# Attention and token-mixing kernel: order of the first q products, of one block's row scaling and of the hand-over to the MLP

## The chip, the cores and the metric

The kernel runs on one core of a Trainium2 chip. The metric is the device time of one execution in microseconds (us), as the median of several runs. Five engines with queues of their own take part: TensorE (PE, with its weight loads PEld), VectorE (DVE), ScalarE (ACT), GpSimd (POOL) and SyncE (SP), which here issues all transfers.

## The reference

For x of 2048 tokens by 640 channels, the output is a gated mix of an attention with 32 heads of width 20 that share one k and one v, and a token-mixing MLP.

```python
S, D, H, Dh, F = 2048, 640, 32, 20, 1728
g = sigmoid((x * gate_w).sum(-1, keepdims=True))
q = (x @ wq) split into 32 heads;  k = x @ wk;  v = x @ wv
a = softmax(q @ k.T * Dh**-0.5) @ v, heads joined, @ wo
h = layernorm(x)                         # over the channels
u = gelu(h.T @ w1 + b1)                  # (D, F): along the tokens
b = (u @ w2 + b2).T
out = g * a + (1 - g) * b
```

## The kernel before, in words

Every float32 operand of a product is split into a high part, which is rounded, and a low part, the rest; a product is then three matmuls (high by high, high by low, low by high). Engines run their instructions in exactly the order in which the source issues them (`manual_schedule`), so each line's place in the Python is its place in the queue. Waits between engines come from the tiles: a reader waits for the writer, and a new user of a buffer waits for the last reader of the old one, transfers included.

**Projection stage (to about 101 us).** Four blocks `sb` of 512 tokens. `load_x` fills `xin[sb % 2]` (tiles `xa`, `xb`). `transpose_x` (L269) turns each of the five column blocks `c` of x on TensorE; `split_x` (L264) makes its high part on ACT and its low part on VectorE. `project` (L276) forms k, v and the gate's sum in one group (`wkv_s`, ten matmuls) and then five q tiles `m` of 128 columns, 15 matmuls each. `split_q` (L290) splits a finished q tile, ACT first and VectorE behind it, into `qh` and `ql`, buffers of the pool `paw` with two of each, and stores both to `q_scr` in memory. It is called one q tile late (`due`). `layer_norm(sb)` (L220) is a generator that the q loop advances with `next`: statistics on VectorE, the reciprocal root partly on GpSimd, and then for each of four row tiles a scaled `ht` on VectorE (L244, pool `tmp`, two buffers), its high part on ACT (L248) and its low part on GpSimd (L249).

Block 0 has its own start, `first_block` (L344). While x and the weights still arrive column block by column block, `turn(c)` casts the weights on GpSimd, transposes and splits x; `first_q` (L340) adds the high-weight products of column block `c` to the first three q tiles at once (`ahead`), three matmuls with the high part of x (`j = 0`) and three with the low part (`j = 1`). `turn(c + 1)` stands in front of `first_q(c, ...)`. Six matmuls on a constant, at L182, come first of all. `gates()` (L328) turns the gate's sums of all four blocks into the columns that the output stage uses: one exponential on ACT and five small VectorE operations.

**First MLP stage (about 101 to 175 us).** The pool `psb` is opened, and ten of the 28 tiles of the first MLP product run (`pu`, L557), in 160 chunk steps of six matmuls. Between them `lead()` issues pairs of products `ms` (L447) whose row maxima VectorE takes (`mp`, L450); softmax needs them. There are 48 leads, spread evenly from step `skip` on:

```python
at, skip, last = 0, 5, NS * PRO - 6
done = [max(0, min(x, last) - skip) * LEAD // (last - skip) for x in (at, at + 1)]
```

A finished tile goes through `gelu` (L483), whose steps are handed out one per chunk step by `pop_chain`. The products `ms` use PSUM banks that the projection stage's `pp` tiles had, and the tile `yo` of `gelu` lies where pool `pa`, with `xin`, had been. `w1_upto` (L112) loads the MLP's weights (`wr`) and splits them on ACT (`wh`, L121) and GpSimd (`wl`, L124).

**Long loop (from about 175 us).** Scores, exponentials, the value product, the other 18 tiles of the first MLP product, the whole second one and the output projection are interleaved by hand. The diff doesn't touch it.

Of the kernel before, what the change touches and what calls it, by code (L numbers as in the profile page):

```python
# [10 lines left out]
F32R = mybir.dt.float32r  # L11
# [6 lines left out]
P = 128  # L18
S, D, H, DH, F = 2048, 640, 32, 20, 1728
NS = S // P  # L20
DC = D // P
FC = (F + P - 1) // P
FT = F - (FC - 1) * P
HD2 = D // 2
NB = 512
NQB = S // NB
NQ = H // 4
NU = NQB * NQ
PRO = 10
# [8 lines left out]
def mix_kernel(ctx: ExitStack, tc: tile.TileContext, A_x, A_wq, A_wk, A_wv, A_wo,  # L38
               B_x, B_w1, B_b1, B_w2, B_b2, gate_w, out):
    nc = tc.nc  # L40
# [3 lines left out]
    def f32(ap):  # L44
        return ap.bitcast(F32)
# [11 lines left out]
    kst = const.tile([P, S], F32R, name="kst")  # L57
# [108 lines left out]
    with tc.tile_pool(name="pa", bufs=1) as pa, \  # L166
# [5 lines left out]
        xin = [pa.tile([P, 4, D], F32, name=name) for name in ("xa", "xb")]  # L172
# [7 lines left out]
        warm = psa.tile([P, NB], F32, name="pp")  # L180
# [39 lines left out]
        def layer_norm(sb):  # L220
            blk = [xts[4 * sb + i] for i in range(4)]
            st4 = paw.tile([P, 4, 2, 6], F32, name="st4")
            mv = paw.tile([P, 4, 2], F32, name="mv")
            for i in range(4):
                for j in range(2):
                    nc.vector.bn_stats(st4[:, i, j, :], blk[i][:, j * HD2:(j + 1) * HD2])
                nc.vector.bn_aggr(mv[:, i, :], st4[:, i])
                if i % 2:
                    yield
            ve = paw.tile([P, 4], F32, name="ve")  # L230
            r0 = paw.tile([P, 4], F32, name="r0")
            r1 = paw.tile([P, 4], F32, name="r1")
            rstd = paw.tile([P, 4], F32, name="rstd")
            nc.vector.tensor_scalar_add(ve, mv[:, :, 1], EPS)
            nc.gpsimd.tensor_tensor(r0, ve, mhalf, op=ALU.pow)
            yield
            nc.vector.tensor_mul(r1, r0, r0)
            nc.vector.tensor_mul(r1, r1, ve)
            nc.vector.tensor_scalar(r1, r1, -0.5, 1.5, op0=ALU.mult, op1=ALU.add)
            nc.vector.tensor_mul(rstd, r0, r1)  # L240
            for i in range(4):
                st = 4 * sb + i
                ht = tmp.tile([P, D], F32, name="ht")
                nc.vector.tensor_scalar(ht, blk[i], mv[:, i, 0:1], rstd[:, i:i + 1],  # L244
                                        op0=ALU.subtract, op1=ALU.mult)
                for d in range(2):
                    hd = ht[:, d * HD2:(d + 1) * HD2]
                    nc.scalar.activation(h_hi[d][:, st, :], hd, AF.Copy)  # L248
                    nc.gpsimd.tensor_sub(h_lo[d][:, st, :], hd, f32(h_hi[d][:, st, :]))  # L249
                yield  # L250

        xT = {}
# [35 lines left out]
                    [(wq_lo[:, c, cols], ts[c][0]) for c in (0, 3, 1, 4, 2)]]  # L288

        def split_q(sb, m, pp):  # L290
            qh = paw.tile([P, NB], F32R, name="qh")
            ql = paw.tile([P, NB], F32R, name="ql")
            nc.scalar.activation(qh, pp, AF.Copy)
            nc.vector.tensor_sub(ql, pp, f32(qh))
            for j, t in enumerate((qh, ql)):
                nc.sync.dma_start(out=q_scr[j, m * P:(m + 1) * P, sb * NB:(sb + 1) * NB], in_=f32(t))
# [43 lines left out]
        def first_q(c, j, ahead):  # L340
            for m, pp in enumerate(ahead):
                nc.tensor.matmul(pp, wq_hi[:, c, m * P:(m + 1) * P], xT[0, c][j], start=c == 0 and j == 0, stop=False)  # L342

        def first_block():  # L344
            ahead = [psa.tile([P, NB], F32, name="pp") for _ in range(QW // P)]

            def turn(c):
                nc.gpsimd.tensor_copy(wq_hi[:, c, :QW], wqs[c])
                split_x(*transpose_x(0, (c,))[0])

            turn(0)
            for c in range(DC):
                if c + 1 < DC:
                    turn(c + 1)
                for j in range(2):
                    first_q(c, j, ahead)
                wq_low(c, slice(0, QW), wqs[c])
            load_x(1)
            split_wkv()
            for c in range(DC):  # L360
                nc.scalar.activation(wq_hi[:, c, QW:], wqs2[c], AF.Copy)
            for c in (0, 3, 1, 4, 2):
                wq_low(c, slice(QW, D), wqs2[c])
            norm = layer_norm(0)
            for _ in range(3):
                next(norm)
            return ahead, norm

        due = None
        for sb in range(NQB):  # L370
            ahead, norm = first_block() if sb == 0 else ([], layer_norm(sb))
            ts = [xT[sb, c] for c in range(DC)]
            pk = project([(wkv_s[:, c, :], t) for c in range(DC) for t in ts[c]])
            if due:
                split_q(*due)
            kv, k_hi, k_lo = split_kv(pk)
            if 0 < sb < NQB - 1:
                load_x(sb + 1)
            store_k(sb, k_hi, k_lo)
            if sb:  # L380
                next(norm)
            for m in range(DC):
                turned = []
                if sb + 1 < NQB and m > 1 and (sb, m) != (2, DC - 1):
                    turned = transpose_x(sb + 1, ((0, 1), (2, 3), (4,))[m - 2])
                p = q_parts(m, ts)
                if m < len(ahead):
                    pp = project(p[2], ahead[m])
                elif m < DC - 1:
                    pp = project(p[0] + p[1] + p[2])  # L390
                else:
                    pp = project([p[r][c] for c in range(DC) for r in range(3)])
                if m:
                    split_q(*due)
                due = sb, m, pp
                if m == 0:
                    turn_v(sb, kv)
                for t in turned:
                    split_x(*t)
                if sb == 1 and m == 1:  # L400
                    turn_bias()
                if sb == 1 and m == 0:
                    w1_load(3)
                if sb == 2 and 0 < m < 4:
                    w1_upto(m)
                if sb == 3 and m == 1:
                    w1_upto(4)
                    new_qmax(0)
                if sb == 3 and m == 2:
                    gates()  # L410
                for _ in range(1 + (sb and m > 1 or sb == 3)):
                    next(norm, None)
            if sb == 2:
                for t in transpose_x(3, (4,)):
                    split_x(*t)
# [118 lines left out]
            f()  # L534

    with tc.tile_pool(name="psb", bufs=2, space=PSUM, side="right") as psb:
        at, skip, last = 0, 5, NS * PRO - 6
        one_by_one[0] = True

        def lead():  # L540
            for b in range(2):
                ms_next(b)()
            ms_done()

        for fc in range(PRO):
            pu = [psb.tile([P, NB], F32, name=f"pu{r}") for r in range(2)]
            for hf in range(4):
                w1_upto(4 * fc + hf + 4)
                if fc and q_parts_due:
                    q_parts_due.pop(0)()  # L550
                wh, wl = w1t.pop(4 * fc + hf)
                for c in range(HS):
                    st = hf * HS + c
                    for k, (w, h) in enumerate(((wh, h_hi[0]), (wh, h_lo[0]), (wl, h_hi[0]))):
                        for r in range(2):
                            rows = slice(64 * r, 64 * r + 64)
                            nc.tensor.matmul(pu[r][:, :HD2], w[rows, c, :], h[rows, st, :],  # L557
                                             start=(st == 0 and k == 0), stop=(st == NS - 1 and k == 2))
                    done = [max(0, min(x, last) - skip) * LEAD // (last - skip) for x in (at, at + 1)]
                    if done[1] > done[0]:  # L560
                        lead()
                    at += 1
                    pop_chain()
                if fc == 1 and hf == 0:
                    new_q(0)
                if fc == PRO - 2 and hf == 2:
                    assert not q_parts_due
                    one_by_one[0] = False
                    fetch_max(0)
            gelu(0, fc, pu)  # L570
            if fc == PRO - 3:
                store_max(0)
# [28 lines left out]
    last = {"half": None, "ins": None, "sig": None}  # L601
# [272 lines left out]
    for i, (steps, rest, done) in enumerate(seq):  # L874
        item, j = divmod(i + 1, 5)
        rest.insert(0, lambda c=4 * (PRO + item) + (48 * j // 5) // 12: w1_upto(c + 4))
    b2 = [b2_jobs(st) for st in range(NS)]
    m = len(seq)
# [105 lines left out]
    for c in range(CUT // P, DC):  # L984
        r = min(P, HEAD - c * P)
        for st in held:
            oT, _ = room(8 + st - (NS - 4))
            for d in range(2):
# [3 lines left out]
                for k, (j, w) in enumerate(((0, wo_hi), (1, wo_hi), (0, wo_lo))):  # L992
                    nc.tensor.matmul(accs[st, d][:, :HD2], oT[:r, j, c, :], w[:r, c, d * HD2:(d + 1) * HD2],
                                     start=(k == 0 and c == CUT // P), stop=False)
# [4 lines left out]
    for i in range(4):  # L999
        st = NS - 4 + i  # L1000
        for d in range(2):
            at = pp_pool.tile([P, NB], F32, name="p")
# [34 lines left out]
```

## Time and profile before

| | before |
|---|---|
| runs | 1703.98, 1704.21, 1705.4 us |
| median | 1704.21 us |
| profiled execution | 1706.32 us |
| its span, first to last instruction | 1704.5 us |
| mean granted TensorE clock | 0.998 |
| instructions | 39051 |

The span is the profiled execution's time without what lies in front of the first and behind the last instruction, 1.8 us. In the profile `L244` is a line of the kernel's source; a row of the timeline gives the start in us, the duration in us, the engine, the line, the operation, `out<-in` with shapes, the count, and in brackets the idle time of the engine before it with what ended it.

### The profile page before, as it was taken

How to read it: one execution, taken by the hardware profiler on the slowest of the kernel's cores; microseconds unless marked ns; L12 is line 12 of the kernel's file. 1: busy time of each engine (PE TensorE's matmuls, PEld its weight loads, DVE VectorE, ACT ScalarE, POOL GpSimd, SP SyncE). 2: the span in 40 equal slices, each digit the busy share in tenths (PEclk: the TensorE clock that was granted, in tenths of full speed). 3: DMA queues.
4: the chain of work that ended last, by engine and by line, in shares of the span. 5: the costliest groups of instructions: out<-in, count | busy, mean ns of one | idle time of the engine just before them, and what ended most of it. 6: DMA issues, size and time to landing. Idle time of an engine off the chain costs nothing.

```text
span 1704.5 us, 39051 instructions
## 1 busy us (share of the span) xinstructions
PE 1693.6 (99%) x14863; PEld 1105.1 (65%) x14863; DVE 1433.5 (84%) x2915; ACT 1189.2 (70%) x2322; POOL 571.0 (34%) x723
## 2 busy tenths in 40 slices
PE   8999999999999999999999999999999999999998
PEld 6889766666666666666666666666666666555666
DVE  5679888888888988888888888888888888888734
ACT  4445577777777777777777777777777777777775
POOL 5467645444444444322222212222221111111200
PEclk9999999999999999999999999999999999999999
DMA  6655322222222222121122222221111222345411
GB/s 187 207 166 144 107 59 69 60 72 70 58 70 64 74 61 75 51 57 53 46 68 70 67 62 62 62 56 54 55 47 41 62 62 64 88 116 145 131 56 57
DMA packets 173377, 135.45 MB, mean 79 GB/s; under 512 B 32729, under 2 KB 139382, under 8 KB 173190
## 3 DMA queue, kind: packets, MB, share of 16 engines
q1 hardware_dynamic: 173190, 132.96, 27.8%
q8 instruction: 117, 1.92, 0.5%
q14 instruction: 70, 0.57, 0.1%
HBM read 100.27 MB, written 31.65 MB: 77 GB/s over the span
## 4 chain that ended last, share of the span: by engine, by line
PE 94%; issue 2%; DVE 2%; DMA 1%; ACT 1%; POOL 0%; SPq 0%; POOLq 0%; DVEq 0%; ACTq 0%
PE o L640 30%; PE s L613 18%; PE ms L447 17%; PE g L685 12%; PE g L848 8%; PE pu L557 3%; PE pp L281 3%; PE g L797 2%; PE ms L754 1%; PE pp L342 0%; DVE mp L450 0%; PE pt L273 0%; ACT slot L248 0%; DMA xa<-in_A_x_dram 0%; PE g L754 0%
## 5 line engine op out<-in xcount | busy, mean ns | idle before, releaser
L450 DVE TENSOR_REDUCE mp<-ms 128x1 f32<-128x512 f32 x2048 | 1278.4, 684 | 170.2 <-PE ms L447 167.7
L616 ACT ACTIVATE p<-s 128x512 f32<-128x512 f32 x2048 | 1069.1, 604 | 397.4 <-PE s L613 393.8
L447 PE MATMUL ms<-kst,qmx 60*128 60x512 f32 x2048 | 848.5, 421 | 1.7 <-DVE mp L450 0.9
L613 PE MATMUL s<-qst,kst 62*128 62x512 f32 x2048 | 745.3, 404 | 0.0
L640 PE MATMUL o<-p,v_sb 128*32 128x512 f32 x4096 | 554.9, 604 | 0.0
L447 PEld LDWEIGHTS ms<-kst,qmx 60*128 60x128 f32 x2048 | 379.4, 185 | 214.7 <-DVE flag L626 182.8
L613 PEld LDWEIGHTS s<-qst,kst 62*128 62x128 f32 x2048 | 378.0, 186 | 11.5 <-issue 10.9
L848 PE MATMUL g<-slot,wh 64*128 64x320 f32 x1152 | 281.3, 318 | 0.0
L124 POOL TENSOR_TENSOR wl<-wr,wh 128x512 fp32r<-128x512 f32 (+1 forms) x176 | 221.3, 1260 | 34.4 <-ACT wh L121 17.9
L123 POOL CAST wh<-wr 128x512 fp32r<-128x512 f32 (+1 forms) x136 | 79.9, 588 | 445.9 <-PE g L685 282.5
L848 PEld LDWEIGHTS g<-slot,wh 64*128 64x128 f32 x1152 | 190.5, 184 | 59.9 <-DVE flag L626 59.9
L685 PE MATMUL g<-slot,wh 64*128 64x320 f32 x864 | 209.0, 317 | 0.0
L685 PE MATMUL g<-u,wh 64*128 64x320 f32 x864 | 208.9, 317 | 0.0
L640 PEld LDWEIGHTS o<-p,v_sb 128*32 128x32 f32 x4096 | 93.7, 108 | 137.6 <-issue 130.3
L848 PE MATMUL g<-slot,wl 64*128 64x320 f32 x576 | 179.3, 311 | 0.0
L685 PEld LDWEIGHTS g<-slot,wh 64*128 64x128 f32 x864 | 142.3, 184 | 40.2 <-DVE flag L626 40.2
L685 PEld LDWEIGHTS g<-u,wh 64*128 64x128 f32 x864 | 142.2, 184 | 40.3 <-DVE flag L626 40.3
L685 PE MATMUL g<-slot,wl 64*128 64x320 f32 x432 | 134.9, 313 | 0.0
L685 PE MATMUL g<-u,wl 64*128 64x320 f32 x432 | 134.8, 312 | 0.0
L848 PEld LDWEIGHTS g<-slot,wl 64*128 64x128 f32 x576 | 106.0, 184 | 15.1 <-DVE flag L626 15.1
L685 PEld LDWEIGHTS g<-slot,wl 64*128 64x128 f32 x432 | 79.5, 184 | 13.4 <-DVE flag L626 13.4
L685 PEld LDWEIGHTS g<-u,wl 64*128 64x128 f32 x432 | 79.5, 184 | 13.4 <-DVE flag L626 13.4
(191 smaller groups left out, 1416.8 us busy)
## 6 DMA issues: line engine op xcount, KB each, us to landing
wr<-in_B_w_dram SPq DMA_DIRECT2D x152, 256.0 KB
qmx<-q_scr SPq DMA_DIRECT2D x192, 80.0 KB
qst<-q_scr SPq DMA_DIRECT2D x192, 80.0 KB
q_scr<-qh SPq DMA_DIRECT2D x20, 256.0 KB
q_scr<-ql SPq DMA_DIRECT2D x20, 256.0 KB
y_scr<-yo SPq DMA_DIRECT2D x16, 320.0 KB
slot<-o_scr SPq DMA_DIRECT2D x16, 320.0 KB
o_scr<-oh SPq DMA_DIRECT2D x124, 40.0 KB
```

The costliest lines, as they stand in the source:

```text
L123: nc.gpsimd.tensor_copy(wh, wr)
L124: nc.gpsimd.tensor_sub(wl, wr, f32(wh))
L281: nc.tensor.matmul(pp, w, t, start=first and n == 0, stop=not more and n == len(steps) - 1)
L447: nc.tensor.matmul(ms, qmax[n][64 * b:64 * b + 60, pr, qt * P:(qt + 1) * P], kst[64 * b:64 * b + 60, kq * NB:(kq + 1) * NB], start=True, s ...
L450: nc.vector.tensor_reduce(mtiles[n][:, c, kq:kq + 1], ms, axis=AX.X, op=ALU.max)
L557: nc.tensor.matmul(pu[r][:, :HD2], w[rows, c, :], h[rows, st, :], start=(st == 0 and k == 0), stop=(st == NS - 1 and k == 2))
L613: nc.tensor.matmul(s, kst[64 * b:64 * b + 62, kb * P:(kb + 1) * P], q[64 * b:64 * b + 62, pr, :], start=True, stop=True)
L616: nc.scalar.activation(p, s, AF.Exp, scale=SCALE)
L640: nc.tensor.matmul(o[32 * hh:32 * hh + 32, :], v_sb[:, kb, :], ptiles.pop((u, hh)), start=(kb == 0), stop=(kb == NS - 1), skip_group_check ...
L685: other_tile(half, nc.tensor.matmul(hold["p"][:, :HD2], w[r, fc % HS, :], u[d][r, fc, :], start=(hold["n"] == 1), stop=(hold["n"] == 6 * F ...
L797: other_tile(half, nc.tensor.matmul(hold["p"][:, :HD2], o[r, c, :], w[r, c, d * HD2:(d + 1) * HD2], start=(hold["n"] == 1), stop=(hold["n" ...
L848: other_tile(half, nc.tensor.matmul(hold["p"][:, :HD2], w[r, st % HS, :], h[d][r, st, :], start=(hold["n"] == 1), stop=(hold["n"] == 6 * NS)))
```

## The change

It has four parts.

1. In `first_block`, for column block 0 only, two more matmuls on the constant and then the three products `first_q(0, 0)` are issued ahead of `turn(1)`; only `first_q(0, 1)` stays behind it.
2. In `layer_norm` of block 0, `ht` of row tile `i + 1` is made at the end of step `i`, behind the ACT and GpSimd instructions of tile `i`. The other blocks keep their order.
3. The last q tile (block 3, `m = 4`) is split into the first two rows of `xin[0]` in place of buffers of `paw`, and `gates()` is called at `m == 3` in place of `m == 2`.
4. `skip` is 3 in place of 5, so the 48 leads spread over 151 steps rather than 149 and begin two steps earlier.

```diff
@@ layer_norm
-            for i in range(4):
-                st = 4 * sb + i
+            hts = []
+
+            def scaled(i):
                 ht = tmp.tile([P, D], F32, name="ht")
                 nc.vector.tensor_scalar(ht, blk[i], mv[:, i, 0:1], rstd[:, i:i + 1],
                                         op0=ALU.subtract, op1=ALU.mult)
+                hts.append(ht)
+
+            ahead = sb == 0
+            if ahead:
+                scaled(0)
+            for i in range(4):
+                if not ahead:
+                    scaled(i)
                 for d in range(2):
-                    hd = ht[:, d * HD2:(d + 1) * HD2]
+                    hd = hts[i][:, d * HD2:(d + 1) * HD2]
+                    st = 4 * sb + i
                     nc.scalar.activation(h_hi[d][:, st, :], hd, AF.Copy)
                     nc.gpsimd.tensor_sub(h_lo[d][:, st, :], hd, f32(h_hi[d][:, st, :]))
+                if ahead and i < 3:
+                    scaled(i + 1)
                 yield
@@ split_q
-            qh = paw.tile([P, NB], F32R, name="qh")
-            ql = paw.tile([P, NB], F32R, name="ql")
+            if (sb, m) == (NQB - 1, DC - 1):
+                qh, ql = (xin[0][:, i, :NB].bitcast(F32R) for i in range(2))
+            else:
+                qh = paw.tile([P, NB], F32R, name="qh")
+                ql = paw.tile([P, NB], F32R, name="ql")
@@ first_block
             for c in range(DC):
+                if c == 0:
+                    for i in range(2):
+                        nc.tensor.matmul(warm, kst[:, :P], kst[:, :NB], start=True, stop=True)
+                    first_q(c, 0, ahead)
                 if c + 1 < DC:
                     turn(c + 1)
-                for j in range(2):
+                for j in range(c == 0, 2):
                     first_q(c, j, ahead)
@@ the q loop
-                if sb == 3 and m == 2:
+                if sb == 3 and m == 3:
                     gates()
@@ the first MLP stage
-        at, skip, last = 0, 5, NS * PRO - 6
+        at, skip, last = 0, 3, NS * PRO - 6
```

## The prediction

> **What bounds the kernel now.** I read the page first: span and busy time by engine.
>
> ```profile
> span 1704.5 us, 39051 instructions
> PE 1693.6 (99%) x14863; PEld 1105.1 (65%) x14863; DVE 1433.5 (84%) x2915; ACT 1189.2 (70%) x2322; POOL 571.0 (34%) x723
> ```
>
> TensorE is busy for 1693.6 of 1704.5 us. So time can be lost or won in only two ways: PE waits, or PE works at a lower clock. Second view: for whom PE waited in the first 200 us, which hold every line the diff touches.
>
> ```profile
> PE pp L281 <- ACT xT_hi L266: 1.4, 1, 1.4
> PE pt L273 <- DMA xa<-in_A_x_dram: 1.0, 1, 1.0
> PE ms L447 <- DVE mp L450: 0.9, 2, 0.6
> PE ms L447 <- DVE ql L294: 0.7, 1, 0.7
> PE pp L281 <- DVE xT_lo L267: 0.3, 1, 0.3
> ```
>
> The columns are total, times, longest. The waits are few and single: one at the start for x (1.0), one for the fifth column of the second x block (1.4 + 0.3), one for the last q tile (0.7), and 0.9 for the running row maxima. The diff has a part for each of the first three. Third view: busy time and granted clock by stretch.
>
> ```profile
> 2.60:6.02 3.42, 2.61 (x9) 1.71 (x7) 0.14 (x1) 0.60 (x1) 1.69 (x5) 1.00 0.84 252
> 6.02:9.43 3.41, 3.24 (x10) 2.76 (x11) 1.25 (x2) 0.60 (x1) 2.41 (x4) 1.00 1.07 323
> 32.25:42.44 10.19, 8.44 (x30) 5.98 (x29) 6.18 (x13) 3.88 (x9) 3.10 (x4) 0.83 0.80 219
> 33.33:36.74 3.41, 1.66 (x7) 0.81 (x6) 2.03 (x5) 2.29 (x5) 1.68 (x2) 1.00 0.32 116
> 36.74:40.15 3.41, 3.41 (x9) 2.64 (x10) 2.49 (x7) 1.22 (x2) 0.62 (x1) 0.50 1.08 235
> 58.98:65.23 6.25, 6.25 (x30) 4.83 (x28) 3.34 (x8) 2.01 (x4) 1.57 (x2) 1.00 0.82 258
> 214.00:1500.00 1286.00, 1286.00 (x11349) 799.72 (x11349) 1140.50 (x2333) 946.09 (x1846) 409.29 (x541) 1.00 0.23 63
> ```
>
> After the stretch's limits and length come busy times of PE, PEld, DVE, ACT and POOL, then the clock. From 214 to 1500 us PE has no idle time and the full clock, so what is gained ahead of 214 us arrives at the end undiminished. And the 1.7 us wait near 35 us costs more than itself: PE is busy for only 1.66 of the 3.41 us up to 36.74, and the next 3.41 us run at clock 0.50, that is, 1.71 us of work is lost on top.
>
> **The first column blocks.** Rows of the timeline:
>
> ```profile
> 5.25 0.60 ACT L266 ACTIVATE slot<-pt 128x512 fp32r<-128x512 f32 x1 [3.26 <-PE pt L273]
> 6.19 1.11 PE L273 MATMUL pt<-ident,xa 128*128 128x128 f32 x4 [0.97 <-DMA xa<-in_A_x_dram]
> 6.95 2.77 PE L342 MATMUL pp<-slot,wq_hi 128*128 128x512 f32 x6
> 9.56 0.60 PE L273 MATMUL pt<-ident,xa 128*128 128x128 f32 x4
> 9.92 1.64 PE L342 MATMUL pp<-slot,wq_hi 128*128 128x512 f32 x6
> ```
>
> The same six products take 2.77 us at 6.95 and 1.64 at 9.92; the four transposes 1.11 and 0.60. So PE is at low clock until about 9.4, though the clock column reads 1.00 there (no clock change is recorded before). The stretch 2.60 to 6.02 had PE busy 2.61 of 3.42 (76%) and was followed by low clock; 6.02 to 9.43 had 3.24 of 3.41 (95%) and was followed by full clock. The change adds two matmuls of 128x512, about 2 x 2.77/6 = 0.92 us by the cold row of the same shape, in an idle gap of 0.97, and three products as soon as ACT is done at 5.85. They fill the first stretch. The two extra matmuls are hidden by the wait for x; without that cover they cost 0.92 (0.55 at full clock).
> If full clock then starts at 6.02: three products to 6.7, transposes to 7.3, three products to 8.1, and the third column's transposes start there rather than at 9.56, 1.5 earlier. I take 1.35, since later steps also hang on ACT, VectorE and the loads. If the stretch still isn't enough, the first transposes of column two are late by three cold products (1.4 us) less the gap filled, but all six products come before the next transposes either way: 0. Ends: -1.35 and +0.3; I take -1.35, since 95% is what the row with the lift shows.
> [...]
>
> **The rows scaled one step ahead.** In the first block `layer_norm` made each `ht` on VectorE in the step that uses it, behind the splits of x:
>
> ```profile
> 29.50 0.61 DVE L244 TENSOR_SCALAR ht<-xa,mv,rstd 128x640 f32<-128x640 f32 x1
> 30.14 0.83 ACT L248 ACTIVATE slot<-ht 128x320 fp32r<-128x320 f32 x2 [1.50 <-DVE ht L244]
> 31.35 1.07 ACT L266 ACTIVATE slot<-pt 128x512 fp32r<-128x512 f32 x2
> 31.49 0.69 DVE L294 TENSOR_TENSOR ql<-pp,qh 128x512 fp32r<-128x512 f32 x1 [1.39 <-ACT qh L293]
> 32.10 1.28 DVE L267 TENSOR_TENSOR slot<-pt,slot 128x512 fp32r<-128x512 f32 x2
> 32.25 2.12 PE L281 MATMUL pp<-slot,wkv_s 128*128 128x512 f32 x8
> 33.93 0.83 ACT L248 ACTIVATE slot<-ht 128x320 fp32r<-128x320 f32 x2 [1.50 <-DVE ht L244]
> 35.15 0.59 ACT L266 ACTIVATE xT_hi<-pp 128x512 fp32r<-128x512 f32 x1
> ```
>
> and, of the waits of ACT from 20 to 42 us,
>
> ```profile
> ACT slot L248 <- DVE ht L244: 6.9, 4, 2.7
> ```
>
> This is a ring: ACT splits x (31.35), VectorE follows (32.10), then makes `ht`, and ACT has waited 1.50 for it, with the q split and the next x split queued behind. One turn is 33.93 - 30.14 = 3.79 us. With `ht` made a step earlier the ring opens: ACT's own work in a turn is 3.79 - 1.50 = 2.29, VectorE's 0.69 + 1.28 + 0.61 = 2.58, and the slower sets the pace. By the last row ACT waited 6.9 us for `ht` in all; the longest wait, 2.7 for the first `ht`, stays. Three turns win 3.79 - 2.58 = 1.2 each at most, 3.6 in all, so `xT_hi` of 35.15 starts between 31.5 and, with half a turn lost to other work, 32.8. PE comes to it at 32.25 + 2.12 = 34.37. The wait goes with 1.5 us or more to spare, and the low clock behind it goes too. `ht` has two buffers; the third waits for GpSimd to finish the first, which is a step behind: nothing.
> Price: the same work, from the first kv product to the start of the second full q tile, takes 10.19 us in block one and 6.25 in block two, where PE is never idle: -3.94. The lower end is that without the low-clock share: 3.94 - 1.71 = -2.23. What is late next is PE itself, as in block two.
> Against it speaks this pair of rows:
>
> ```profile
> 77.94 2.20 DVE L244 TENSOR_SCALAR ht<-xa,mv,rstd 128x640 f32<-128x640 f32 x2
> 77.97 1.30 POOL L124 TENSOR_TENSOR wl<-wr,wh 128x512 fp32r<-128x512 f32 x1
> ```
>
> Two scalings beside a GpSimd subtraction took 2.20, twice 0.61 alone: 0.98 lost. Moved ahead, `ht` may fall beside GpSimd's subtractions of the row before. Three `ht`, at most 0.5 lost each, are 1.5 us, about the margin.
> [...]
>
> **The last q tile, the gates and the leads.**
>
> ```profile
> 96.61 0.47 DVE L331 TENSOR_SCALAR ez<-ez 128x16 f32<-128x16 f32 x1
> 98.11 1.13 DVE L244 TENSOR_SCALAR ht<-xb,mv,rstd 128x640 f32<-128x640 f32 x2
> 100.20 1.06 ACT L293 ACTIVATE qh<-pp 128x512 fp32r<-128x512 f32 x2
> 103.30 0.60 ACT L293 ACTIVATE qh<-pp 128x512 fp32r<-128x512 f32 x1 [2.03 <-DMA q_scr<-qh]
> 105.61 0.69 DVE L294 TENSOR_TENSOR ql<-pp,qh 128x512 fp32r<-128x512 f32 x1 [3.50 <-DMA q_scr<-ql]
> 106.35 0.67 PE L447 MATMUL ms<-kst,qmx 60*128 60x512 f32 x2 [0.66 <-DVE ql L294]
> 111.33 0.51 ACT L487 ACTIVATE yo<-pu,bias 128x320 f32<-128x320 f32 x1
> 108.44 1.29 DVE L450 TENSOR_REDUCE mp<-ms 128x1 f32<-128x512 f32 x2 [0.26 <-PE ms L447]
> 122.55 1.51 DVE L497 SCALAR_TENSOR_TENSOR yo<-yo 128x320 f32<-128x320 f32 x1
> 125.18 0.48 DVE L503 SCALAR_TENSOR_TENSOR yo<-yo 128x320 f32<-128x320 f32 x1
> ```
>
> The last `qh` and `ql` wait for the store of an earlier tile (2.03, 3.50), because `paw` has two buffers of each; until `ql` is read out, the first lead product at 106.35 has no PSUM bank. In `xin[0]`, unused since block two was scaled, both splits run as soon as their product is done. The gates, 98.11 - 96.61 = 1.5 us on VectorE, move from ahead of the last two `ht` to ahead of the last two `ql`; queued behind them are these, the first reductions, and on SP the stores. Worked forward: without the gates the two `ht` start near 96.6, take 1.13, and end by 98.5 if GpSimd gives up a buffer 0.8 late; ACT's last pair of copies (0.83 as above) ends near 99.4, its next q split near 100.0; VectorE ends that `ql` near 100.7, the gates near 102.2, two more `ql` at 0.69 near 103.6. The first reader of a gate comes in the long loop behind 214 us, so the gates themselves cost nothing.
> `skip` 3 instead of 5 puts the first lead two chunk steps earlier. PE was ready for it at 106.35 - 0.66 = 105.69. The row at 108.44 gives the spacing of leads, 1.29 + 0.26 = 1.55 us for three chunk steps with a pair of products, at most 0.5 a step, so it becomes due at about 104.7. 103.6 is early enough by 1.1: -0.66, or 0 if the gates run that late. The matmuls are the same in number. The stores on SP come two us earlier, and so do the weight loads queued behind them. The first gelu step (111.33) writes where `xin[0]` lay and must wait for these stores; issued by about 104 and landing within the 3.5 us that the row above shows for one, they are done by 107.5: nothing.
> With 48 leads over 151 steps instead of 149, each falls elsewhere against gelu. The waits of 0.9 in the second fence come from a late reduction, behind such a row as 122.55 (1.51, where its like at 125.18 takes 0.48). I leave them as they are; ends -0.9, and up to +1 for each further such collision.
>
> **The sum.** -1.35 - 3.94 - 0.66 = -5.95. The profiled execution took 1706.32 us (span 1704.5 and 1.8 around it), so it would take 1700.4. The three runs' median, 1704.21, lies 2.11 lower. If that is only what profiling costs, the median becomes 1704.21 - 5.95 = 1698.3; if those runs merely met fewer low-clock stretches, the change removes 2.11 less from them and the median becomes 1700.4. I can't tell these apart and forecast the middle, 1699.4.
>
> **Rivals.** First, the low-clock stretches aren't what the timed runs lose: only waits go. 2.23 + 0.66 = 2.9, so 1704.21 - 2.9 = 1701.3. [...] Against: the profile has both stretches. Chance 0.18.
> [...] Chance 0.07.
> Third, slower: the leads realign. The nine gelu tiles have two VectorE steps each (cube and product) with GpSimd's weight splits beside them, 18 in all; a collision costs VectorE 1.51 - 0.48 = 1.0 and its slack between leads is 0.26. From six collisions that reach PE in full, 6 x 1.0, the gain of 5.95 is eaten; at ten, 1704.21 + 4.1 = 1708.3. Against: before, PE lost 0.9 there in all. Chance 0.05.
>
> **How the numbers follow.** The forecast case, 1697 to 1700.8, has the other 0.70. About 0.2%, 3.4 us, is what a measurement of this kernel can tell from no change: faster means below 1700.8, slower above 1707.6. The forecast gives faster 0.70; the first two rivals lie within it: same 0.25; slower 0.05. The range runs from 1698.3 - 0.9 = 1697.4, with the maxima's waits gone too, to the first rival with 0.6 for an unhidden start or tail, 1701.9.
>
> **What would show it.** Right: six products of the first column at about 1.6 us and no wait near 6; no PE wait for `xT_hi` or `xT_lo`, clock 1.00 throughout 33 to 40 us, the block-one stretch at 6.3 us; the last `ql` done by 104 and the first lead without a wait. Wrong: ACT still waiting for `ht` in turns of 3.8 us, VectorE rows of 1.5 us in number between 105 and 175 with PE waiting for `mp`, or all waits gone and the time within 3.4 us of before, which would leave only that the three runs never had the low clock.

## The result

| | before | changed |
|---|---|---|
| median of nine runs each | 1704.41 us | 1699.78 us |
| lowest to highest | 1703.3 to 1706.77 | 1699.55 to 1701.0 |
| profiled execution | 1706.32 | 1699.95 |
| its span | 1704.5 | 1698.2 |

The ratio is 0.9971, 95% interval 0.9961 to 0.9981: faster by 4.6 us or 0.3%, against 1699.4 forecast in 1697.4 to 1701.9. The scatter shrank as well, from 3.5 us to 1.5.

The page of the changed kernel and PE's waits in its first 200 us:

```profile
span 1698.2 us, 39056 instructions
PE 1690.9 (100%) x14865; PEld 1102.9 (65%) x14865; DVE 1434.7 (84%) x2915; ACT 1190.0 (70%) x2322; POOL 570.8 (34%) x723
```

```profile
PE pp L182 <- DVE kst L63: 1.4, 1, 1.4
PE ms L466 <- DVE mp L469: 0.5, 2, 0.4
PE pt L333 <- DVE kv L316: 0.2, 1, 0.2
```

(Lines of the changed source stand up to 19 further down: L466 is `ms`, L245 `ht`, L309 `ql`, L293 the projections, L357 `first_q`.) The waits for x, `xT_hi`, `xT_lo` and `ql` are gone; what remains is 0.5 us for row maxima and what both kernels have. The list of the weight loads has one more, ahead of the transposes of block two's x:

```profile
PEld pt L285 <- DMA xa<-in_A_x_dram: 0.2, 1, 0.2
```

Stretches, with the columns explained in the prediction:

```profile
2.60:6.02 3.42, 3.42 (x12) 2.27 (x10) 0.14 (x1) 0.60 (x1) 1.69 (x5) 1.00 0.90 259
30.82:37.08 6.26, 6.26 (x31) 4.83 (x29) 4.53 (x10) 2.13 (x5) 1.86 (x2) 1.00 0.89 241
208.00:1494.00 1286.00, 1286.00 (x11353) 799.35 (x11345) 1140.76 (x2331) 946.06 (x1846) 408.98 (x540) 1.00 0.23 63
```

PE is busy throughout the first one, where it was 76% (in this execution the clock rose at 6.46, and PE is busy for 3.42 of the 3.42 us ahead of that as well); the work of block one that took 10.19 us takes 6.26; the long loop is as it was. The timeline of the start, then of the first block's rows:

```profile
4.87 1.20 PE L370 MATMUL pp<-kst 128*128 128x512 f32 x2
5.99 1.16 PE L357 MATMUL pp<-slot,wq_hi 128*128 128x512 f32 x3
6.99 0.60 PE L285 MATMUL pt<-ident,xa 128*128 128x128 f32 x4
7.34 0.95 PE L357 MATMUL pp<-slot,wq_hi 128*128 128x512 f32 x3
8.13 0.60 PE L285 MATMUL pt<-ident,xa 128*128 128x128 f32 x4
15.02 2.03 PE L293 MATMUL pp<-slot,wkv_s 128*128 128x512 f32 x8
...
24.48 1.16 DVE L245 TENSOR_SCALAR ht<-xa,mv,rstd 128x640 f32<-128x640 f32 x1
27.17 0.86 POOL L259 TENSOR_TENSOR slot<-ht,slot 128x320 fp32r<-128x320 f32 x1
27.35 1.03 DVE L245 TENSOR_SCALAR ht<-xa,mv,rstd 128x640 f32<-128x640 f32 x1
29.11 0.84 ACT L258 ACTIVATE slot<-ht 128x320 fp32r<-128x320 f32 x2
30.31 0.62 ACT L278 ACTIVATE xT_hi<-pp 128x512 fp32r<-128x512 f32 x1
31.34 0.68 DVE L279 TENSOR_TENSOR xT_lo<-pp,xT_hi 128x512 fp32r<-128x512 f32 x1
32.69 0.40 PE L293 MATMUL pp<-xT_hi,wkv_s 128*128 128x512 f32 x1
```

The first kv product starts at 15.02 (before: 16.45, by the trace's records). The first column's six products take 1.16 + 0.95 = 2.11 us, with the rise of the clock in their midst. The last `ht`, at 27.35, is 1.8 us ahead of the copies that use it, at 29.11, and these follow what is in front of them without a gap. `xT_hi` is done at 30.93 for a PE that comes at 32.69. Of the four waits of ACT for `ht` from 20 to 42 us, 6.9 us before, only that for the first `ht` is left:

```profile
ACT slot L258 <- DVE ht L245: 2.7, 1, 2.7
```

The hand-over:

```profile
92.97 1.15 DVE L245 TENSOR_SCALAR ht<-xb,mv,rstd 128x640 f32<-128x640 f32 x1 [0.77 <-POOL slot L259]
96.12 0.44 DVE L346 TENSOR_SCALAR ez<-ez 128x16 f32<-128x16 f32 x1
97.86 0.68 DVE L309 TENSOR_TENSOR xa<-pp,xa 128x512 fp32r<-128x512 f32 x1
99.49 0.39 PE L466 MATMUL ms<-kst,qmx 60*128 60x512 f32 x2
104.80 0.51 ACT L506 ACTIVATE yo<-pu,bias 128x320 f32<-128x320 f32 x1
```

The 0.77 in the first row is the late buffer that the forecast allowed for. The last `ql` (into `xa`) ends at 98.54 and the first lead follows at 99.49 without a wait. Nor does the first gelu step, at 104.80, wait for the stores out of `xa`.

Set side by side, the two spans (1704.53 and 1698.17) differ by 6.36 us, and by stage as follows (starts of the named matmuls in the two traces): start to first kv product 16.45 and 15.02, -1.43; to block one's first kv product 15.80 both, 0; from there to block two's 26.73 and 23.00, -3.73; to the first MLP product 42.48 both, 0; to the first score product of the long loop 85.70 and 84.44, -1.26; to the end 1517.37 and 1517.43, +0.06. (In the trace before, the first MLP stage runs to about 186 us, not the 175 named at the start.)

### The profile page after: what moved, and what is told of

Same layout as the page of the kernel before. It is cut to its first block, busy times and chain, and to the rows that moved or that the text cites. A ratio compares the mean times of both kernels' runs of the same rounds, so it can differ in the third digit from the quotient of the medians.

```text
span 1698.2 us, 39056 instructions
## 1 busy us (share of the span) xinstructions
PE 1690.9 (100%) x14865; PEld 1102.9 (65%) x14865; DVE 1434.7 (84%) x2915; ACT 1190.0 (70%) x2322; POOL 570.8 (34%) x723
## 4 chain that ended last, share of the span: by engine, by line
PE 97%; issue 2%; DVE 1%; POOL 0%; ACT 0%; POOLq 0%; DVEq 0%; ACTq 0%
PE o L659 30%; PE s L632 18%; PE ms L466 17%; PE g L704 12%; PE g L867 8%; PE pp L293 4%; PE pu L576 4%; PE g L816 2%; PE ms L773 1%; PE pt L285 0%; PE pp L357 0%; DVE mp L469 0%; PE g L773 0%; PE pp L182 0%; PE pp L285 0%
## 5 line engine op out<-in xcount | busy, mean ns | idle before, releaser
L466 PE MATMUL ms<-kst,qmx 60*128 60x512 f32 x2048 | 847.5, 421 | 0.7 <-DVE mp L469 0.5
L466 PEld LDWEIGHTS ms<-kst,qmx 60*128 60x128 f32 x2048 | 378.0, 185 | 213.4 <-DVE flag L645 176.9
```

Of the source, the lines that this page charges most:

```text
L466: nc.tensor.matmul(ms, qmax[n][64 * b:64 * b + 60, pr, qt * P:(qt + 1) * P], kst[64 * b:64 * b + 60, kq * NB:(kq + 1) * NB], start=True, s ...
```

## The experiments

For the clock I use one more reading, the trace's own records of when the granted clock changes. "Full from" is the first record of full clock, "low" a later stretch at half clock (one more, behind the last products, from 1702.44 us in before and from 1696.06 in changed, is left out); kv0 is the start of the first kv product, "block one" the stretch that took 10.19 us before; all in us. Busy shares ahead of a rise or a fall are taken over 3.41 us, the length of the low stretches in the table.

| kernel | full from | kv0 | low | block one | span |
|---|---|---|---|---|---|
| before | 9.43 | 16.45 | 36.74 to 40.15 | 10.19 | 1704.5 |
| before, again | 5.29 | 15.52 | 36.01 to 39.42 | 10.18 | 1703.7 |
| start only | 5.44 | 14.77 | 36.16 to 39.57 | 10.20 | 1703.1 |
| rows only | 5.80 | 14.97 | none | 6.25 | 1699.7 |
| tail only | 5.38 | 14.97 | 36.09 to 39.51 | 10.17 | 1702.5 |
| gap filled | 4.61 | 14.82 | none | 8.61 | 1701.9 |
| two matmuls | 6.62 | 15.16 | none | 8.63 | 1702.3 |
| changed | 6.46 | 15.02 | none | 6.26 | 1698.2 |
| no fill | 4.62 | 14.54 | none | 6.26 | 1697.9 |
| skip 5 | 4.28 | 14.41 | none | 6.26 | 1698.5 |
| gates back | 6.78 | 15.11 | none | 6.26 | 1699.2 |
| load ahead | 6.82 | 15.14 | none | 6.26 | 1698.1 |
| cold start | 9.28 | 16.11 | none | 6.26 | 1699.5 |

My theory was that the change is a sum of three separate gains, two of them with a share of low clock; the rivals stand with each experiment. The experiments ran against runs of the kernel before of their own, whose median was 1705.5 us in the first set, 1706.61 in the second and 1706.68 in the third; the ratios are to those.

**The parts by themselves.** Part 1, the loop of `first_block` as in the change:

```diff
+                if c == 0:
+                    for i in range(2):
+                        nc.tensor.matmul(warm, kst[:, :P], kst[:, :NB], start=True, stop=True)
+                    first_q(c, 0, ahead)
...
-                for j in range(2):
+                for j in range(c == 0, 2):
```

> Part 1 of the change alone (two extra matmuls and the early first q products). [...] Rival, the change works as a whole (what the start gains is given back at the wait for xT_hi near 34 us, since ACT and VectorE set that date): the wait for xT_hi grows from 1.4 to about 2.8 us and the time is that of before within 0.3 us.

Measured: 1704.43 us, ratio 0.9994 (0.9985 to 1.0003), not clear of no change. Of its waits,

```profile
PE pp L281 <- ACT xT_hi L266: 1.4, 1, 1.4
PE ms L451 <- DVE ql L294: 0.9, 1, 0.9
```

the one for `xT_hi` is 1.4 as before, so an earlier start isn't given back there; the rival's 2.8 is ruled out. What the part does to the median stays open between a gain of 2.6 us and a loss of 0.5.

Part 2, `ht` one step ahead in block 0:

```diff
+            if ahead:
+                scaled(0)
...
+                if ahead and i < 3:
+                    scaled(i + 1)
```

> Part 2 alone (rows of the first block scaled one step ahead). Theory: the waits of 1.4 and 0.3 us for xT_hi and xT_lo and the low-clock stretch behind them vanish, the stretch from the first kv product of block one to its second full q tile takes 6.3 us instead of 10.2, and the median falls by 2.2 to 3.9 us. Rival, the ring isn't opened by this alone but by the earlier start: some of the wait stays (over 0.5 us) and the median falls by under 1.5 us.

Measured: 1702.11 us, ratio 0.9981 (0.9972 to 0.999), so 3.2 us (1.7 to 4.8). The block-one stretch is

```profile
30.79:37.04 6.25, 6.25 (x30) 4.83 (x28) 3.87 (x9) 2.02 (x4) 1.29 (x1) 1.00 0.93 232
```

The ring is opened by this edit alone. Of its waits one stands out, that for the last `ql`, 1.1 us where the kernel before had 0.7 and 1.0 in its two traces:

```profile
PE ms L459 <- DVE ql L306: 1.1, 1, 1.1
```

Parts 3 and 4 together:

```diff
+            if (sb, m) == (NQB - 1, DC - 1):
+                qh, ql = (xin[0][:, i, :NB].bitcast(F32R) for i in range(2))
...
-                if sb == 3 and m == 2:
+                if sb == 3 and m == 3:
...
-        at, skip, last = 0, 5, NS * PRO - 6
+        at, skip, last = 0, 3, NS * PRO - 6
```

> Parts 3 and 4 alone (last q tile in xin[0], gates one q tile later, skip 3). Theory: the wait of 0.7 us ahead of the first lead goes and the waits for the row maxima stay within 0.2 to 1.2 us; the median falls by 0.3 to 1.3 us, hardly more than can be told from no change. Rival, the place of the leads is what matters in the first MLP stage: the waits for row maxima go to zero or over 2 us and the median moves by over 1.5 us either way.

Measured: 1705.01 us, ratio 0.9996 (0.9987 to 1.0005): as expected too small for the median. In its trace the wait for `ql` is gone and that for row maxima 0.8; the first MLP stage, from its first product to the first score product, takes 85.06 us, 0.64 less than before (the six traces with the old hand-over have 85.33 to 85.71). The three medians' ratios leave 1.0, 3.2 and 0.7 us, together 4.9, near the whole; but each is uncertain by 1.5 us, so this sum agrees with separate gains and doesn't show them. The traces do that, stage by stage.

**Wait and clock, apart.**

```diff
+            if sb == 1:
+                pk = project(kv_steps[:8], more=True)
+                fill = pst.tile([P, NB], F32, name="pt")
+                for i in range(6):
+                    nc.tensor.matmul(fill, wq_hi[:, 0, :P], wq_hi[:, 0, P:P + NB], start=True, stop=True)
+                pk = project(kv_steps[8:], pk)
```

> The kernel before with nothing of the change, but with six matmuls of 128x512 on weights put in front of the ninth kv product of block one, where TensorE waits 1.4 us for xT_hi; their result is not used. They take 6 x 0.23 = 1.4 us. Theory, wait and clock are two costs: xT_hi comes no earlier (kv product nine starts near 35.8 us as before), but no low-clock stretch follows, the stretch of block one takes 8.5 us instead of 10.2 or a little more, and the median falls by up to 1.7 us, as often as the low clock occurs in the kernel before. Rival, the low clock isn't caused by the idling: the stretch stays at 10.2 us with the clock at 0.5 and the time stays that of before or rises.

Measured: 1705.23 us, ratio 0.9997 (0.9989 to 1.0006). Its timeline, its block-one stretch, and the same stretch of the kernel with part 1 alone:

```profile
32.58 1.55 PE L378 MATMUL pt<-wq_hi 128*128 128x512 f32 x6
34.16 0.50 PE L281 MATMUL pp<-xT_hi,wkv_s 128*128 128x512 f32 x1
```

```profile
30.65:39.26 8.61, 8.25 (x37) 5.95 (x36) 6.15 (x13) 3.87 (x9) 3.15 (x4) 1.00 0.76 210
```

```profile
30.64:40.84 10.20, 8.45 (x30) 5.99 (x29) 6.18 (x13) 3.90 (x9) 3.12 (x4) 0.83 0.80 226
```

The product that needs `xT_hi` starts 3.51 us behind the first, as before (3.53), so `xT_hi` comes no earlier; the stretch is 1.58 us shorter, at clock 1.00 instead of 0.83. That splits the 3.94 us: 1.6 for the low clock, 2.35 for the waits. The median moved by only 0.5 us (-1.9 to +1.0), so what the low clock costs the median stays open, and the next kernel shows that the filling wasn't needed in every execution.

```diff
+                if c == 0:
+                    for i in range(2):
+                        nc.tensor.matmul(warm, kst[:, :P], kst[:, :NB], start=True, stop=True)
```

> The kernel before with the two extra matmuls behind the first transposes only; the order of the first q products is that of before. [...] Rival, the early products are what is needed: the first six products still take about 2.8 us and the first kv product starts near 16.4 us.

Measured: 1704.95 us, ratio 0.9991 (0.9981 to 1.0), not clear of no change. Rows of its start, then the 3.41 us up to full clock and two stretches about its wait for `xT_hi`, which it still has:

```profile
4.87 1.20 PE L355 MATMUL pp<-kst 128*128 128x512 f32 x2
6.26 0.81 PE L273 MATMUL pt<-ident,xa 128*128 128x128 f32 x4 [0.20 <-DMA xa<-in_A_x_dram]
6.83 1.63 PE L342 MATMUL pp<-slot,wq_hi 128*128 128x512 f32 x6
```

```profile
3.21:6.62 3.41, 3.21 (x11) 2.06 (x11) 0.69 (x1) 0.60 (x1) 1.09 (x3) 1.00 0.85 253
30.51:33.92 3.41, 2.58 (x11) 1.62 (x9) 2.10 (x4) 1.92 (x6) 1.34 (x2) 1.00 0.43 154
33.92:37.34 3.42, 2.50 (x10) 1.83 (x11) 2.66 (x5) 1.68 (x5) 0.96 (x2) 1.00 0.79 236
```

The six first products take 1.63 with the old order, so the early products aren't needed; that rival falls. Unfilled starts often get an early lift too (the table), so this one trace doesn't show that the two matmuls brought the rise at 6.62. That they did is my estimate: the 3.41 us up to it are 94% busy with them, and 2.36 of 3.41 us or 69% without their rows, less than the 76% that low clock followed in the kernel before. And the same 1.75 us of idling, nothing filled in, brought no low clock here: in the last two rows PE is busy for 2.58 of 3.41 and 2.50 of 3.42 us, and the clock is 1.00. In the four traces with a fall (before twice, start only, tail only), PE was busy for 1.65 or 1.66 of the 3.41 us that ended at it, as in before, again:

```profile
32.60:36.01 3.41, 1.65 (x6) 0.83 (x5) 2.03 (x4) 2.29 (x5) 1.69 (x2) 1.00 0.31 113
36.01:39.42 3.41, 3.41 (x9) 2.65 (x8) 2.65 (x7) 1.23 (x2) 1.00 (x1) 0.50 1.09 242
```

48% busy, then half clock. Why the clock stayed at 1.00 in two matmuls is not shown.

**The start, once more.** First without the two matmuls:

```diff
-                    for i in range(2):
-                        nc.tensor.matmul(warm, kst[:, :P], kst[:, :NB], start=True, stop=True)
```

> The changed kernel without the two extra matmuls; the early first q products stay. TensorE then idles about 0.7 us between 5.2 and 5.9 us. [...] Rival, the order alone is enough: the first kv product starts at 15.0 to 15.2 us and the median stays that of the changed kernel within 0.3 us.

Measured: 1699.95 us over five runs (1699.71 to 1701.73). The profiled execution had full clock from 4.62 us, ahead of its 0.8 us of idling, so it doesn't show whether the order alone is enough when the clock rises later, and five runs don't show the two matmuls to be needed beside the early products.

Then with hardly anything in the start:

```diff
-        for i in range(6):
+        for i in range(1):
             nc.tensor.matmul(warm, kst[:, :P], kst[:, :NB], start=True, stop=True)
...
-                    for i in range(2):
-                        nc.tensor.matmul(warm, kst[:, :P], kst[:, :NB], start=True, stop=True)
```

> The changed kernel with its start left idle: one matmul on the constant instead of six at the start, and none of the two extra ones; the early first q products stay. Theory, the date of full clock sets the start term: the clock lifts only near 9.4 us or later, the first kv product starts at 16 to 17.5 us instead of 15.0, the later parts are as in the changed kernel, and the median is 1.2 to 2.5 us above the changed kernel's 1699.8. Rival, the order of the products is what made the gain: the first kv product starts by 15.3 us and the time stays within 0.4 us of the changed kernel's.

Measured: 1701.6 us (1701.29 to 1702.36), 1.7 above load ahead (below) of the same set, whose highest, 1700.46, lies under the lowest here; 1.8 above the changed kernel of the first runs.

```profile
5.64 1.62 PE L357 MATMUL pp<-slot,wq_hi 128*128 128x512 f32 x3 [0.78 <-ACT slot L278]
7.77 1.63 PE L357 MATMUL pp<-slot,wq_hi 128*128 128x512 f32 x3
9.60 1.64 PE L357 MATMUL pp<-slot,wq_hi 128*128 128x512 f32 x6
16.11 2.03 PE L293 MATMUL pp<-slot,wkv_s 128*128 128x512 f32 x8
```

Three products take 1.62 us up to 9.3 and six take 1.64 after it. A late lift costs 1.1 us of kv0 with the early products in place (16.11 to 15.02) and 1.5 with the old order (before to tail only, 16.45 to 14.97): the date of full clock sets the start term, not the order alone.

The kernel before, profiled once more:

> The kernel before once more, for one further look at its two low-clock stretches. [...] Rival, the dates belong to the kernel: full clock at 9.4 us and low clock from 36.7 to 40.2 us as before.

```profile
6.76 0.66 PE L273 MATMUL pt<-ident,xa 128*128 128x128 f32 x4 [1.54 <-DMA xa<-in_A_x_dram]
7.17 1.63 PE L342 MATMUL pp<-slot,wq_hi 128*128 128x512 f32 x6
```

Full clock came at 5.29 us this time, as the idle gap began, so the dates don't belong to the kernel and the rival falls. (This execution was on another chip; but on the first one tail only and gap filled, with the same start, had full clock from 5.38 and 4.61.) But x landed 0.6 us later than in the first trace, and kv0 was 15.52. Pairs with an equally early lift show what the early products are worth then: start only and tail only (lift at 5.44 and 5.38) have kv0 at 14.77 and 14.97, no fill and gap filled (4.62 and 4.61) at 14.54 and 14.82, that is 0.2 to 0.3 us.

**The hand-over's pieces.**

```diff
-        at, skip, last = 0, 3, NS * PRO - 6
+        at, skip, last = 0, 5, NS * PRO - 6
```

> The changed kernel with skip 5 instead of 3. Theory: the last split is early enough for either, so the first lead has no wait in both; only the places of the leads against the gelu steps differ, the waits for row maxima lie between 0.2 and 1.5 us, and the median is that of the changed kernel within 0.8 us. Rival, skip is a gain of its own: the median is over 1 us above the changed kernel's.

Measured: 1700.31 us (1699.7 to 1701.12). No wait ahead of the first lead; the waits for row maxima are 0.9 us instead of 0.5, and the first MLP stage takes 84.84 us, where the five other traces of the changed kernel and its variants have 84.30 to 84.45. In the median such 0.4 us can't be told.

```diff
-                if sb == 3 and m == 3:
+                if sb == 3 and m == 2:
                     gates()
```

> The changed kernel with the gates at m == 2 again, as before the change. Theory, the buffers of the last q tile are what removes the wait and the gates' place is free: the last ql ends no later against the start of the first MLP stage than in the changed kernel (2.2 us behind it), the first lead has no wait, and the median is the same within 0.3 us. Rival, the gates' place is what frees VectorE in time: the first lead waits 0.3 to 1 us for ql and the median rises by as much.

Measured: 1700.4 us (1699.93 to 1700.96). The last `ql` starts at 97.67 and ends at 98.36, 1.4 us behind the start of the first MLP stage instead of 2.2 in the changed kernel; the first lead has no wait. So the buffers do it, and the gates' new place is free at best: the first MLP stage takes 84.33 us here. The median is 0.6 above the changed kernel's, where 0.3 was expected; beside it skip 5 has 1700.31 and no fill 1699.95, so with five runs each this can't be told from no change. What does cost this execution 0.5 us is elsewhere:

```profile
PE pt L285 <- DMA xa<-in_A_x_dram: 0.5, 1, 0.5
```

This wait, 0.2 in the weight loads of the changed kernel, comes when PE reaches block two's x before it has landed. It isn't the ring alone that brings it: gap filled and two matmuls, with the ring as before but no low clock, wait 0.2 us there too. So one version further:

```diff
+            if 0 < sb < NQB - 1:
+                load_x(sb + 1)
             if due:
                 split_q(*due)
             kv, k_hi, k_lo = split_kv(pk)
-            if 0 < sb < NQB - 1:
-                load_x(sb + 1)
```

> The changed kernel with one more move: in blocks one and two load_x stands in front of the split of the last q tile instead of behind it, so SP issues the load of the next x block ahead of two stores. In the changed kernel the transposes of block two now wait 0.2 us for x (0.5 us in the run with the gates moved back), a wait that the kernel before did not have. Theory: the load starts about 2 us earlier and this wait goes; the time falls by 0.2 to 0.5 us, too little to be told by the median, so the profile decides. Rival: the load takes the transfers from the q stores, ACT and VectorE wait longer for their buffers, and a wait of the same size or larger comes up elsewhere ahead of 100 us.

Measured: 1699.9 us (1699.39 to 1700.46), ratio to before 0.9961 (0.9949 to 0.9974). The wait isn't in its list and none came in its place; block one to block two takes 22.78 instead of 23.00 us. But no fill, skip 5 and cold start, with the load in its old place, take 22.78 too: the wait doesn't come in every execution, and one trace without it doesn't show that the move removed it. The kernel beats the one before; from the changed one it can't be told by the time.

## Why the prediction was right

*The start, -1.35:* measured -1.43 between the two profiled executions, with 3.42 of 3.42 us busy where 76% had been. That the two matmuls lift the clock by themselves stays an estimate (above). Full clock was to come at 6.02 and came at 6.46, so the six first products took 2.11 us and not the 1.6 that was named as a sign. The forecast took the start of its one profile, with full clock at 9.43 us, for that of the timed runs and summed the whole term; but in four of five traces of a kernel with the old, unfilled start the lift came by 5.8 us. The term is one for the unlucky execution, and for the median only bounded (above).

*The rows, -3.94:* the stretch went from 10.19 to 6.26, by this edit alone. `xT_hi` was to start between 31.5 and 32.8 on the old time axis; it started 0.51 us ahead of block one's first kv product, that is, 31.74. The feared meeting with GpSimd took place twice, 1.16 us for the `ht` at 24.48 and 1.03 for that at 27.35 instead of 0.61, 1.0 us in all, and stayed inside the margin of 1.5. (The 2.20 us for two `ht` in the prediction were 1.68 and 0.60: a single one had lost it all, so 0.5 each was no bound.) "What is late next is PE itself" was nearly right: 0.2 us for block two's x came up, and of 3.94 the stage kept 3.73.

*The hand-over, -0.66:* mis-sized. The last `ql` was to end at 103.6 on the old axis, 2.1 us behind the start of the first MLP stage; it ended 2.2 behind it. The first lead came 3.19 behind it, 104.65 on the old axis, as worked out. But the stage got shorter by 1.26. The wait for `ql` that the term stands for was 0.7 in the trace that the forecast read, and 0.8 to 1.1 in the five others with the old hand-over. The waits for row maxima, left at 0.9 with -0.9 as an end, fell to 0.5. Whether the leads' new places did that is not shown: traces with the old hand-over have 0.5 to 0.9, tail only 0.8, the five of the changed kind with `skip` 3 0.4 to 0.5, the one with `skip` 5 0.9. Some 0.2 us of the 1.26 stands in no list of waits. (The 3.50 us that the forecast took for the landing of a store are VectorE's idle time ahead of that row, which the landing ends; no wait came of it.) The third rival, more collisions, didn't come.

*The median:* two readings of the 2.11 us between before's profile and its median were left open. The changed kernel's profiled execution, 1699.95, lies 0.2 from its median, so profiling costs next to nothing, and the second reading, 1700.4, is the better one; the stages gained 0.4 more than the sum of 5.95, which makes 1700.0. That the forecast, 1699.4, is only 0.4 from the measured median is luck in part: it is the middle of two readings of which one was wrong. And 1704.21 was itself a lucky median. In later sets the kernel before had 1705.5 to 1706.7, about its profiled 1706.32; beside the latter two, no fill, skip 5, gates back and load ahead come out 6.0 to 6.7 us faster, nearer to 5.95 than the 4.6 above.

The first rival (only waits go, a gain of 2.9) lies just outside the measured 3.2 to 6.6, and the 3.2 (1.7 to 4.8) of rows only covers its 2.23 as well as the 3.94: the medians alone hardly decide. The mean granted clock, which is known for each of the later runs, does. One fall for 3.41 us takes 1.71 / 1704.5 = 0.001 from it; half clock behind the last products, 2.1 us long in the profiles of both kernels, takes 0.0006. So, with an end like theirs, a run at 0.998 had a fall besides. Of 60 runs of the kernel before 32 had 0.998 or less, 26 had 0.999, which leaves it open, and 2 had 1.000, hence none. The 58 runs of the eight kernels in which that idling is gone or filled (rows only, gap filled, the changed kernel and its variants) all had 0.999 or more. The timed runs do meet the low clock, in half of the cases at least; what it costs them is known from the stretch alone (1.6 us), not from a median.

## What to carry to other kernels

A wait of TensorE can have a second price, low clock behind it (here 1.6 us beside 2.35 for the waits), and it is read from the stretch behind the wait, not from the list of waits. Compare the stretch with a twin that has no wait (here block two's, 6.25 us beside 10.19), and treat the clock's share as something that comes in some executions only (here in four of the five traces in which nothing filled or removed the wait): a sum made from one profiled execution holds its own luck. In a ring of in-order engines look for the step that can be issued one turn earlier; here that opened it, 10.19 to 6.25 us in rows only, without any engine getting faster.

## What the runs showed of the hardware

Full clock came first at 4.28 to 9.43 us after the first instruction in the thirteen traces, at 9.43 and 5.29 in the two of the kernel before. In the first of these the records of a change (9.43, 36.74, 40.15, 1702.44) lie 27.307, 3.413 and 1662.291 us apart, 8, 1 and 487 times one length; the two of the changed kernel (6.46, 1696.06) lie 1689.597 us apart, 495 times the same. The four low stretches in the table lasted 3.41 to 3.42 us.

In the kernel before PE was 76% busy from 2.60 to 6.02, and the clock stayed low until 9.43. In rows only it was 83% busy in the 3.41 us up to the rise at 5.80:

```profile
2.39:5.80 3.41, 2.83 (x9) 1.82 (x7) 0.00 (x0) 0.55 (x1) 1.91 (x6) 1.00 0.83 262
```

At full clock PE was 57% busy in 3.41 us right behind the lift (before, again) and 68% busy in 3.42 us of the first MLP stage (two matmuls), and no fall stood right behind either:

```profile
5.29:8.70 3.41, 1.94 (x11) 1.64 (x12) 1.31 (x2) 1.16 (x2) 1.38 (x2) 1.00 1.06 310
102.19:105.61 3.42, 2.32 (x30) 2.06 (x29) 1.31 (x3) 0.63 (x1) 2.52 (x2) 1.00 0.51 156
```

Behind 48% in the 3.41 us up to 36.74 (before) and up to 36.01 (before, again) the clock fell to 0.50. These are single traces; how much idling a rise bears or a fall takes, they do not show. With the idling filled, block one took 8.61 us at clock 1.00 where it took 10.19 at 0.83, so half clock for 3.41 us cost 1.6.

The median of the kernel before moved from 1704.4 to 1706.7 us between the sets of runs, that of the changed kernel and its near variants only from 1699.8 to 1700.4. The landing of x (0.6 us apart in the two traces of before), the wait for the last `ql` (0.7 and 1.0 there) and the date of full clock (9.43 and 5.29) vary in the traces and could do this; which of them did was not tried.
